# A decode kernel's query weight loaded in three pieces that split the 128 rows into 16 and 112, and a bias loaded in one transfer

## The chip, the cores and the metric

The kernel runs on one core of one Trainium2 chip. The metric is device time in microseconds of one execution, the median over several runs. A profile is taken of one execution; its "span" reaches from the first to the last instruction and is a little shorter than the time of the execution.

The core has five engines with queues of their own: PE (matrix multiply), DVE (vector), ACT (scalar functions), POOL and SP. SP and ACT also issue transfers (DMAs) between device memory and the on-chip memory, which has 128 rows (partitions). The transfers are carried out by 16 DMA engines.

## What is computed

One decode step of a block that adds attention over a sliding window of cached keys and values and a squared-ReLU MLP to its input. The batch is 2, one token each, the model width 576.

```python
xn = layernorm(x)                                   # 2 x 576
# attention: 32 query heads on 16 key/value heads of width 128
q = xn @ wq                                         # 576 x 4096
k, v = k_cache[:, :, Sk-W:], v_cache[:, :, Sk-W:]   # last W = 2048 of 8192 places
o = softmax(q k^T / sqrt(128)) v
att = o @ wo                                        # 4096 x 576
# MLP
h = relu(xn @ w1 + b1) ** 2                         # 576 x 4608
mlp = h @ w2 + b2                                   # 4608 x 576
out = x + att + mlp
```

All tensors are bf16. Each weight and each cached byte is used once, 53.6 MB in all.

## The kernel before

**The work.** The cache is cut into eight units: four groups of four key/value heads, for each of the two batch entries. A unit's keys are one load of 128 rows x 16,384 B (2 MB, `load_k`), its values another (`load_v`). `step(u)` transposes the unit's keys on PE (`transposes`), copies them out of PSUM on ACT and DVE (L273, L275), multiplies them with the queries (`scores`), and takes the softmax; the product with the values of unit `u - 2` (`pv`) is put between the transposes. The loop over `u` runs from 2 to 6, with `mlp_h` (the first half of the MLP) ahead of the last step.

**The weights.** `issue_flat` loads a weight as one flat run of bytes, cut into 128 equal rows: row p of the tile holds the p-th part. For wq a row is 18,432 elements, 36,864 B. `q_rows` multiplies in 36 matmuls, nine values of `t` times four of `g`; the matmul for `t` reads the columns from `2048 t` to `2048 t + 2047` of all 128 rows. wq, w1 and wo take turns in one buffer (`wbig`, one buffer).

**Order of the transfers.** All large loads go through SP's queue in this order: wq (two pieces, columns 0 to 4095 and 4096 to 18,431), k_0, k_1, v_0, k_2, v_1, k_3, then v_2 and k_4 and so on as buffers come free (six buffers for keys and values, so v_2 takes the place of k_0), w1 after v_5, wo after `mlp_h`, and at the end w2 in five pieces. ACT's queue has the small ones: x at the start, b1 (two transfers of four rows each, L420) and b2 (L421). b1 is wanted only in `mlp_h`, b2 in the first `out_acc`.

**What orders an issue.** The instruction stream of each engine is put in order by a scheduler: the b1 and b2 issues, which are written after the first softmax, stand in ACT's stream ahead of the `rstd` activation. Each transfer reports its end on one of eight counters, handed out in turn over all queues. A transfer's issue waits until the transfer that had the counter before it has landed, and, where it takes over a buffer, until the last reader of the old contents is done. In the kernel before, the counters 0 to 7 go to x, wq's first piece, wq's second piece, b1's first half, b1's second half, b2, k_0 and k_1; then v_0, k_2, v_1 and k_3 have counters 0 to 3. So k_2 is issued after the landing of wq's first piece, v_1 after that of the second, and k_3 after b1's first half.

Of the kernel before, what the change touches and what calls it, by code (L numbers as in the profile page):

```python
# [16 lines left out]
def kernel(  # L17
# [14 lines left out]
    nc = tc.nc  # L32
    P = 128
# [75 lines left out]
    def load_k(u):  # L109
        issue_kv(k_tiles, A_k_cache, u, "k")  # L110
# [1 line left out]
    def load_v(u):  # L112
        issue_kv(v_tiles, A_v_cache, u, "v")

    def issue_flat(w, name, cuts=()):
        n = w.shape[0] * w.shape[1] // P
        tl = wbig.tile([P, NH * L1], BF16, tag="wbig", name=name)
        w_p = w.rearrange("r n -> (r n)").rearrange("(p l) -> p l", p=P)
        for lo, hi in zip((0,) + cuts, cuts + (n,)):
            nc.sync.dma_start(out=tl[:, lo:hi], in_=w_p[:, lo:hi])  # L120
        return tl

    const.tile([P, 152], F32, name="pad_0")
# [4 lines left out]
    nc.vector.memset(eps_t[:], 1e-5)  # L128
    warm = const.tile([B, 2], F32, name="warm")
    nc.scalar.activation(out=warm[:, 0:1], in_=eps_t[:], func=ACT.Sqrt)  # L130
    wq_sb = issue_flat(A_wq, "wq", (4096,))
    load_k(0)
    load_k(1)
    load_v(0)
# [45 lines left out]
    for t0, half, k0, n, pc in ((0, 0, 0, NK, 0), (0, 1, 0, NK, 1), (1, 0, 1, NK - 1, 1), (1, 1, 0, NK - 1, 0)):  # L180
# [11 lines left out]
                          in_=own[:].unsqueeze(2).to_broadcast([P, NC, WC]))  # L192
# [11 lines left out]
                          in_=ident[0:2 * NG4, 0:2 * NG4].rearrange("p (x g) -> p x g", g=NG4).unsqueeze(3)  # L204
                          .to_broadcast([2 * NG4, 2, NG4, B]))

    b1_sb = const.tile([2 * NG4, HW], BF16, name="b1_sb")
# [208 lines left out]
    softmax(0)  # L416
    load_v(2)
    b1_rows = B_b1.rearrange("(x n) -> x n", n=HW)
    for i0, i1 in ((0, 4), (4, 8)):
        nc.scalar.dma_start(out=b1_sb[i0:i1, :], in_=b1_rows[i0:i1, :])  # L420
    nc.scalar.dma_start(out=xb_sb[B:B + 1, :], in_=B_b2.rearrange("(o n) -> o n", o=1))  # L421
    step(1)
    load_k(4)
# [1 line left out]
    for u in range(2, NU - 1):  # L425
        step(u)
        if u + 1 < NU - 2:
            load_v(u + 1)
        if u == 4:
            w1_sb = issue_flat(B_w1, "w1")  # L430
        if u + 3 < NU:
            load_k(u + 3)
        if u == 5:
            for v in (NU - 2, NU - 1):
                load_v(v)
    mlp_h(w1_sb)
    wo_sb = issue_flat(A_wo, "wo")
    w2a_sb = w2pool.tile([P, FR * D], BF16, name="w2a")
    w2b_sb = kvpool.tile([P, R9 * D], BF16, tag="kv", name="w2b")
# [28 lines left out]
    for r in range(FR):  # L468
        w, o = (w2b_sb, r) if r < R9 else (w2c_sb, r - R9)
# [41 lines left out]
```

## Time and profile before

| | us |
|---|---|
| median of 3 runs (133.61 to 133.85) | 133.74 |
| the profiled execution | 133.6 |
| its span | 131.7 |
| busy in the span: PE / DVE / ACT | 84.6 / 63.1 / 46.6 |
| wq's first piece: issue to landing | 4.8 |
| wq's second piece: issue to landing | 12.9 |
| a key load, median: issue to landing | 25.6 |
| mean granted TensorE clock (1 is full) | 0.883 |

The span holds 53.74 MB of DMA traffic, a mean of 408 GB/s. In the profile a line such as "L93 PE MATMUL q_ps<-wq,xnT 128*4 128x512 bf16 x28" names the line of the code (L93 and L96 are the helpers through which all matmuls and transposes go), the engine, the operation, the output and inputs, the shape and the number of instructions. "SPq" and "ACTq" are issues of transfers on those queues. The chain of waits is followed back from the last instruction to what released it. In the table of stretches, "1.50:2.00 0.50" is a stretch and its length; then come the busy time and count of each engine, the granted clock, the mean busy share of the 16 DMA engines and the GB/s. A packet is counted in one stretch, so shares over 1 occur in short ones.

### The profile page before, as it was taken

The numbers are of one execution on the slowest core, as the hardware profiler recorded it, in microseconds if no ns is written. First come the engines' busy times: TensorE is split into PE (matmuls) and PEld (weight loads), VectorE is DVE, ScalarE is ACT, GpSimd is POOL, SyncE is SP. The second block draws the span as 40 slices with busy tenths as digits, with TensorE's granted clock in tenths as the row PEclk, the third lists the DMA queues.
The fourth block names the chain that finished last, engine by engine and source line by source line (L and its number), as shares of the span: only waits on it lengthen the run. The fifth ranks groups of instructions, "written<-read, shape, count | busy, mean of one in ns | idle before, by whom it ended". The sixth has DMA issues, their size and how long they took to land.

```text
span 131.7 us, 2025 instructions
## 1 busy us (share of the span) xinstructions
PE 84.6 (64%) x818; PEld 46.3 (35%) x818; DVE 63.1 (48%) x176; ACT 46.6 (35%) x68; POOL 4.2 (3%) x14
## 2 busy tenths in 40 slices
PE   0040767985599687699687797003919974629782
PEld 0010236553346353345353353002507631205341
DVE  6760034555447677457677496400073487560000
ACT  6700019497255185265085283200015452000101
POOL 2000000010100100100100100100010001000000
PEclk9999999999779999859999999955586899655799
DMA  4999999999999999999999999999999989899970
GB/s 118 480 419 420 418 443 418 448 418 423 445 413 438 423 443 428 413 458 413 443 423 411 458 490 403 408 431 428 413 443 418 504 381 504 382 416 403 400 286 1
DMA packets 3643, 53.74 MB, mean 408 GB/s; under 512 B 418, under 2 KB 563, under 8 KB 819
## 3 DMA queue, kind: packets, MB, share of 16 engines
q1 hardware_dynamic: 3604, 53.61, 95.6%
q8 instruction: 6, 0.10, 0.3%
q10 hardware_dynamic: 30, 0.02, 0.0%
q14 instruction: 3, 0.02, 0.0%
HBM read 53.62 MB, written 0.00 MB: 407 GB/s over the span
## 4 chain that ended last, share of the span: by engine, by line
DMA 74%; PE 15%; ACT 5%; issue 1%; SPq 1%; DVE 1%; ACTq 0%; DVEq 0%
DMA w<-in_B_w_dram 24%; DMA w2c<-in_B_w_dram 23%; DMA k<-in_A_k_cache_dram 17%; DMA wq<-in_A_wq_dram 10%; PE kT_ps L96 5%; PE h_ps L93 3%; ACT kT L273 3%; PE q_ps L93 2%; PE sc_ps L93 2%; PE o_ps L93 1%; PE out_ps L93 1%; ACT L305 1%; SPq L120 1%; DVE qrow L241 1%; ACT qrow L241 0%
## 5 line engine op out<-in xcount | busy, mean ns | idle before, releaser
L96 PE MATMUL kT_ps<-ident_f,k 128*128 128x128 f32 x256 | 39.0, 295 | 6.7 <-DMA k<-in_A_k_cache_dram 4.2
L273 ACT COPY kT<-kT_ps 128x1024 bf16<-128x1024 bf16 x32 | 31.8, 1012 | 15.3 <-PE kT_ps L96 15.3
L96 PEld LDWEIGHTS kT_ps<-ident_f,k 128*128 128x128 f32 x256 | 29.3, 149 | 21.8 <-issue 7.4
L275 DVE COPY kT<-kT_ps 128x1024 bf16<-128x1024 bf16 x32 | 21.8, 682 | 6.4 <-PE kT_ps L96 5.9
L93 PE MATMUL sc_ps<-kT,qz 128*32 128x512 bf16 x128 | 9.8, 384 | 6.1 <-DVE kT L275 5.5
L305 ACT ACTIVATE p<-sc_ps,bias 128x512 bf16<-128x512 f32 x8 | 5.5, 687 | 21.5 <-DVE gown L301 21.4
L93 PE MATMUL o_ps<-v,pT 128*32 128x512 bf16 x128 | 12.2, 466 | 0.0
L93 PE MATMUL h_ps<-w,xnT 128*4 128x288 bf16 x72 | 4.5, 442 | 8.8 <-DMA w<-in_B_w_dram 8.8
L93 PEld LDWEIGHTS <-xnT 128*4 128x4 bf16 x108 | 3.5, 117 | 18.3 <-issue 15.3
L336 DVE SCALAR_TENSOR_TENSOR o<-o_ps,in_s,o 128x128 f32<-128x128 f32 x24 | 8.2, 344 | 0.4
L308 DVE STREAM_TRANSPOSE pT<-p 128x512 bf16<-128x512 bf16 x8 | 5.7, 709 | 5.6 <-ACT p L305 5.6
L376 DVE TENSOR_TENSOR hrow<-t 100x1152 bf16<-100x1152 f32 x2 | 2.6, 1354 | 10.5 <-ACT t L374 10.5
L93 PE MATMUL q_ps<-wq,xnT 128*4 128x512 bf16 x36 | 4.2, 622 | 5.4 <-DMA wq<-in_A_wq_dram 4.0
L294 DVE TENSOR_REDUCE m<-sc_ps 128x1 f32<-128x512 f32 x8 | 5.5, 691 | 3.4 <-PE sc_ps L93 3.4
L93 PE MATMUL op_ps<-o,of_h 128*32 128x129 f32 x16 | 3.4, 299 | 4.6 <-DVE o L336 4.6
L298 POOL PARTITION_ALL_REDUCE gmax<-m x8 | 2.9, 365 | 92.2 <-DVE m L296 92.2
L93 PEld LDWEIGHTS <-qz 128*32 128x32 bf16 x128 | 2.0, 94 | 9.9 <-DVE kT L275 7.6
L334 DVE TENSOR_SCALAR o<-o_ps,in_s 128x128 f32<-128x128 f32 x8 | 2.7, 343 | 5.3 <-PE o_ps L93 5.3
L96 PE MATMUL pro_ps<-ident,xn_sb 2*128 2x2 bf16 x5 | 0.9, 181 | 6.8 <-DVE xn_sb L171 6.5
L241 ACT CAST qrow<-q_ps 100x512 bf16<-100x512 f32 x1 | 0.6, 585 | 12.1 <-DVE qrow L241 12.1
L463 ACT COPY pre_sb<-pre_ps 34x288 f32<-34x288 f32 x1 | 0.4, 393 | 12.6 <-PE pre_ps L93 12.6
L93 PE MATMUL out_ps<-wo,ws 128*2 128x288 bf16 x32 | 4.0, 441 | 1.1 <-DVE ws L352 1.1
(76 smaller groups left out, 61.4 us busy)
## 6 DMA issues: line engine op xcount, KB each, us to landing
k<-in_A_k_cache_dram SPq DMA_DIRECT2D x8, 2048.0 KB, 25.6
v<-in_A_v_cache_dram SPq DMA_DIRECT2D x8, 2048.0 KB, 22.8
w<-in_B_w_dram SPq DMA_DIRECT2D x1, 5184.0 KB
wo<-in_A_wo_dram SPq DMA_DIRECT2D x1, 4608.0 KB
wq<-in_A_wq_dram SPq DMA_DIRECT2D x1, 3584.0 KB, 12.9
w2a<-in_B_w_dram SPq DMA_DIRECT2D x1, 2592.0 KB
w2b<-in_B_w_dram SPq DMA_DIRECT2D x1, 1296.0 KB, 29.2
wq<-in_A_wq_dram SPq DMA_DIRECT2D x1, 1024.0 KB, 4.8
```

The lines of the kernel that those rows point to most:

```text
L93: tc.keep_in_program_order(nc.tensor.matmul(*a, **k))
L96: tc.keep_in_program_order(nc.tensor.transpose(*a, **k))
L241: cp(out=qrow[:, k * QW:(k + 1) * QW].rearrange("p (i a d) -> p i a d", a=2, d=Dh), in_=q_ps[0:RB, k * QW // 2:(k + 1) * QW // 2].rearrang ...
L273: nc.scalar.copy(out=kT, in_=kT_ps[:])
L275: nc.vector.tensor_copy(out=kT, in_=kT_ps[:])
L294: nc.vector.tensor_reduce(out=m1[:], in_=sc_ps[:], axis=AX.X, op=ALU.max)
L298: nc.gpsimd.partition_all_reduce(gmax[:], m2[:], channels=P, reduce_op=ReduceOp.max)
L305: nc.scalar.activation(out=p_sb[:], in_=sc_ps[:], func=ACT.Exp, bias=bias[:, 0:1], scale=scale, accum_out=o1[:, Dh:Dh + 1])
L308: nc.vector.transpose(out=pT[:].rearrange("p j r -> p (j r)"), in_=p_sb[:])
L334: nc.vector.tensor_scalar(scalar1=in_s[:, 0:1], scalar2=None, op0=ALU.mult, **kw)
L336: nc.vector.scalar_tensor_tensor(scalar=in_s[:, k:k + 1], in1=o1[:, 0:Dh], op0=ALU.mult, op1=ALU.add, **kw)
L376: nc.vector.tensor_tensor(out=h4[:, :, k * HB:(k + 1) * HB], in0=t4, in1=t4, op=ALU.mult)
```

## The change

`issue_flat` takes a pair (rows, columns) in place of a list of cuts. With it, a weight is loaded in three transfers: the first columns of the first rows, then all columns of the other rows, then the rest of the first rows. wq uses (16, 8192), that is 16 rows x 16,384 B, 112 rows x 36,864 B, and 16 rows x 20,480 B. w1 and wo are loaded as before, in one transfer each. b1's eight rows come in one transfer in place of two.

```diff
-    def issue_flat(w, name, cuts=()):
+    def issue_flat(w, name, lead=None):
         n = w.shape[0] * w.shape[1] // P
         tl = wbig.tile([P, NH * L1], BF16, tag="wbig", name=name)
         w_p = w.rearrange("r n -> (r n)").rearrange("(p l) -> p l", p=P)
-        for lo, hi in zip((0,) + cuts, cuts + (n,)):
-            nc.sync.dma_start(out=tl[:, lo:hi], in_=w_p[:, lo:hi])
+        pieces = [(0, P, 0, n)]
+        if lead:
+            p1, c1 = lead
+            pieces = [(0, p1, 0, c1), (p1, P, 0, n), (0, p1, c1, n)]
+        for p0, p1, c0, c1 in pieces:
+            nc.sync.dma_start(out=tl[p0:p1, c0:c1], in_=w_p[p0:p1, c0:c1])
         return tl
...
-    wq_sb = issue_flat(A_wq, "wq", (4096,))
+    wq_sb = issue_flat(A_wq, "wq", (16, 8192))
...
-    for i0, i1 in ((0, 4), (4, 8)):
-        nc.scalar.dma_start(out=b1_sb[i0:i1, :], in_=b1_rows[i0:i1, :])
+    nc.scalar.dma_start(out=b1_sb[:], in_=b1_rows[:, :])
```

In the built program the counters 0 to 7 now go to x, wq's first piece, b1, b2, wq's second piece, wq's third piece, k_0 and k_1. v_0, k_2, v_1 and k_3 again have counters 0 to 3, so k_2 is issued after the landing of wq's first piece, v_1 after b1's and k_3 after b2's. The first matmul of `q_rows` waits for wq's first and second pieces, the seventeenth for the third. The order of the transfers on SP's queue, and all counters from v_2 on, are as before.

## The prediction

> **What bounds the kernel now.** I read the chain of waits first, then the DMA row of the slices, then the stretches of the start and the groups in order of time at both ends.
>
> ```profile
> DMA 74%; PE 15%; ACT 5%; issue 1%; SPq 1%; DVE 1%; ACTq 0%; DVEq 0%
> ...
> DMA  4999999999999999999999999999999989899970
> ```
> ```profile
> q1 hardware_dynamic: 3604, 53.61, 95.6%
> ...
> q10 hardware_dynamic: 30, 0.02, 0.0%
> ```
> Three quarters of the chain that ended last is transfers, and after the first 3.3 us slice the 16 DMA engines are busy in every slice until the work runs out. SP's queue (q1) alone fills 95.6% of them. So the kernel is one stream of 53.6 MB. Its two ends:
>
> ```profile
> 1.18 12.89 DMA wq<-in_A_wq_dram
> ...
> 14.12 3.18 PE q_ps L93 x28
> ...
> 96.95 30.81 DMA w2c<-in_B_w_dram
> ```
> The last weight piece lands at 127.75 us. After it come 1.36 us of matmuls (L470), a 0.39 us copy and the store. Whatever delays the stream delays the end by as much; whatever merely happens earlier on PE or ACT does not move it. The stretches (last two columns: DMA share, GB/s) give the stream's speed:
>
> ```profile
> 1.50:2.00 0.50, 0.00 (x0) 0.00 (x0) 0.44 (x3) 0.50 (x1) 0.00 (x0) 1.00 1.34 185
> 2.00:2.50 0.50, 0.00 (x0) 0.00 (x0) 0.43 (x4) 0.50 (x1) 0.00 (x0) 1.00 0.37 82
> 2.50:3.00 0.50, 0.00 (x0) 0.00 (x0) 0.47 (x3) 0.48 (x3) 0.00 (x0) 1.00 0.73 279
> ...
> 14.00:34.00 20.00, 15.66 (x132) 8.84 (x131) 8.95 (x19) 10.87 (x16) 0.36 (x1) 1.00 1.01 432
> ```
> Full speed is 432 GB/s. From 1.5 to 3.0 us it is 185, 82 and 279, in all 0.273 MB in 1.5 us.
>
> How rows go to engines follows from the packet counts. SP issues 25 transfers of 128 rows and one of 2 rows (the store): 25 x (128 + 16) + 2 + 2 = 3604, so a 128-row transfer is one packet a row and 16 completion writes, one an engine. ACT's queue (q10) moves 2 + 4 + 4 + 1 + 2 + 2 = 15 rows in 30 packets: each row has a completion of its own. A transfer of four rows therefore runs on four engines, one row each, and not on one engine that owns eight neighbouring rows.
>
> **The change, part by part.** Call the three wq pieces A (16 rows x 16,384 B = 262,144 B), B (112 rows x 36,864 B = 4,128,768 B) and C (16 rows x 20,480 B = 327,680 B). The bytes are those of before, 4.72 MB. By the counts above I take A and C as one row an engine and B as seven rows an engine (an estimate; 16 divides both). What is new is the pattern: sixteen engines writing sixteen neighbouring rows at once, and engines that each hold seven neighbouring rows, so that they no longer stand in eight fixed rows each. No row of the trace shows a large transfer that is narrower than 128 rows, so each cost is bounded from the stretches.
>
> A: in the trace the first 262,144 B take 1.5 us less the time of the last 11 KB of the 0.273 MB, about 1.45 us. Low end: one packet an engine in place of two, the whole ramp gone, 0.262 / 432 = 0.61 us, which is 0.84 less. High end: all of it at the slowest half microsecond, 82 GB/s, 3.20 us, which is 1.75 more. Taken: the mean of the first microsecond, (185 + 82) / 2 = 133 GB/s, since A is that stretch: 1.97 us, +0.5.
>
> C: low end 0.328 / 432 = 0.76 us, no loss. High end 82 GB/s, 4.0 us, +3.24. Taken: 133 GB/s, the stretch in which few bytes are under way on each engine, as in C: 2.46 us, +1.7.
>
> B: low end 4.129 / 432 = 9.56 us, as before. High end the half microsecond at 279 GB/s, the mildest of the three slow ones, since B is wide: 14.8 us, +5.2. No row is nearer to one end, so the middle: +2.6.
>
> Sum of the pieces: 0.5 + 1.7 + 2.6 = +4.8 us. There is nothing to absorb it, as the stream is full from 3.0 us to the last landing.
>
> The page "SBUF — State Buffer" of the Trainium skill, section "Door 1: The DMA port swizzle (why `[64,N]` ≈ `[32,N]`)", speaks against the change: how fast a transfer writes depends on how many of 16 ports its partitions reach, and partitions 0 to 15 reach four, for which it measured 104 GB/s. By it A and C, 589,824 B, would take 5.67 us where 432 GB/s gives 1.37, a loss of 4.3 us as an estimate from that page, and the sum with B unharmed would be 137.9. No run here shows it yet.
>
> Edits that cost nothing, each with its cover:
>
> ```profile
> 9.10 1.02 PE L93 MATMUL q_ps<-wq,xnT 128*4 128x512 bf16 x8 [1.37 <-DVE q_ps L225]
> ...
> 14.09 0.54 SPq L105 DMA_DIRECT2D v<-in_A_v_cache_dram  x1
> 14.67 0.60 SPq L105 DMA_DIRECT2D k<-in_A_k_cache_dram  x1
> ...
> 24.19 0.54 SPq L105 DMA_DIRECT2D v<-in_A_v_cache_dram  x1
> ```
> PE's early matmuls. Eight of 36 ran at 9.10 while the second piece was under way. Now the first sixteen wait for A and B, the last twenty for C. At 3.18 / 28 = 0.114 us each, 20 follow C's landing, 2.27 us in place of 3.18, and only if the sixteen (1.8 us) are done by then. That is 0.9 us to be won on PE, not on the stream: the first issue that needs it is v_2 at 24.19, which waits for PE to be done with k_0, and at that time the queue still holds 12.58 MB less (24.19 - 14.08) x 0.432 = 8.2 MB, 19 us of work.
>
> SP's third wq issue: about 0.40 us (two took 0.86), so k_0 is issued at some 2.05 in place of 1.64. wq's bytes cover it until 14.
>
> The completion counters. The program has eight, taken in turn, and a transfer's issue waits for the counter's last user. In the built program k_2 still waits for the first wq piece (A), but v_1 no longer waits for the second wq piece (the issue at 14.09): it waits for the b1 transfer, and k_3 for b2. The total is the same, so from v_2 on each waits as before. Behind those two issues on SP stand only further cache loads. At 14.09 the queue holds four loads, 8.39 MB or 19.4 us, so neither an earlier issue nor one late by up to 19 us moves the stream.
>
> The bias: one issue for two on ACT.
> ```profile
> 4.31 1.28 ACT L165 ACT_TABLE_LOAD   x1
> 4.58 0.61 ACTq L420 DMA_DIRECT2D b_sb<-in_B_b_dram  x2
> 5.22 0.27 ACTq L421 DMA_DIRECT2D xb_sb<-in_B_b_dram  x1
> 5.61 0.29 ACT L165 ACTIVATE rstd<-mv,eps_t 2x1 f32<-2x1 f32 x1
> ```
> The 0.3 us saved lies under the table load that ends at 5.59. Without that cover it would bring rstd 0.3 us earlier, and then the early q matmuls, which now wait for wq anyway. b1 is read at 81.8 us.
>
> Forecast: 133.6 (the profiled execution: span 131.7 and 1.9 around it) + 4.8 = 138.4. The median of the runs shown is 0.14 above that execution, so **138.5**.
>
> **The rivals.**
>
> Faster: the ramp. If narrow writes run at full speed, C and B cost nothing, and A alone decides. For it: the 82 GB/s at 2.0 to 2.5 us, with eight rows queued on each engine; a single packet an engine could come to speed sooner. Against it: the first packet's wait is there whatever its size. Half the ramp's 0.84 us: 133.6 - 0.4 + 0.14 = 133.3 (132.9 to 133.45). It decides as soon as C's 0.33 MB takes less than about 0.9 us.
>
> No change: the bytes, the engines and each engine's share (16,384 + 7 x 36,864 + 20,480 = 8 x 36,864 B) stay, the stream runs at 432 GB/s, and all else lies under it: 133.7. For it: every piece on SP's queue, from 0.15 MB (the last w2c) to 5.3 MB (w1), keeps the stream full. Against it: all those are 128 rows wide.
>
> Slower by more than I say: every doubtful term at its high end, 1.75 + 3.24 + 5.2 = 10.2, gives 143.8; it needs engines to collide through all of B.
>
> That the change does not do what it says is ruled out by the built program, which has the three pieces and the one bias transfer.
>
> **How the numbers follow.** A measurement here can tell 0.2%, 0.27 us, from no change. Forecast (slower) 0.62, its own range 135.0 to 142.0: the taken A and C with nothing for B give 133.74 + 2.2 = 135.9, of which I allow a mis-sizing of 0.9; the top is B at its high end with A and C as taken, 141.1, and as much again. The worst sum (slower too) 0.08, the ramp (faster) 0.20, no change 0.10. The predicted time is that of the likeliest. From 133.2 to 142.0 some 0.08 is left out above and some 0.10, half of the faster case, below.
>
> **What would show it.** Queue 1 with 3604 - 288 + (16 + 16) + (112 + 16) + (16 + 16) = 3508 packets if rows are dealt as I say; 3484 if A and C stay on four engines. Slow stretches of DMA, well under 432 GB/s, up to wq's last landing, which moves from 14.08 to about 18.9 and takes w2c's landing from 127.75 to about 132.5 with it. From then on 432 GB/s and the same distances between landings. If wq lands at 14 or sooner, the terms for B and C were wrong; if it lands late but w2c does not, the claim that the stream has no slack was.

## The result, and the profile after

The changed kernel took 143.93 us (median of 6 runs, 143.4 to 144.3) against 133.73 us before (6 runs, 133.53 to 133.85): the ratio is 1.0762, with a 95% interval of 1.0747 to 1.0777. It is slower by 10.2 us, and the prediction of 138.5 us with a range up to 142.0 missed it.

The rate by slices of the kernel before (3.29 us each), and of the kernel after (3.55 us each) the DMA row, the rate, the packets of SP's queue and the chain of waits:

```profile
GB/s 118 480 419 420 418 443 418 448 418 423 445 413 438 423 443 428 413 458 413 443 423 411 458 490 403 408 431 428 413 443 418 504 381 504 382 416 403 400 286 1
```
```profile
DMA  9969997999999999999999999999999999899970
GB/s 178 228 177 324 260 170 175 424 424 443 438 424 427 429 424 424 438 434 429 434 420 424 436 443 490 409 437 403 415 434 424 446 451 467 374 431 423 399 296 3
...
q1 hardware_dynamic: 3508, 53.61, 95.8%
...
DMA 79%; PE 11%; ACT 3%; issue 2%; SPq 2%
```

The DMA digits are nearly as high as before, yet for the first seven slices, some 25 us, the engines move 170 to 324 GB/s. Before, they moved 418 to 480 from the second slice on. The busy digit hardly shows this: a packet under way counts as busy however slowly it moves. Only the GB/s row does. The 3508 packets are the number worked out beforehand, so A, B and C are each spread over sixteen engines: one row an engine for A and C, seven for B. Which rows each engine got, the count does not say.

The stretches of the kernel after (busy time of PE, PEld, DVE, ACT and POOL, the clock, then the DMA share and GB/s):

```profile
5.00:8.00 3.00, 0.90 (x5) 0.49 (x5) 1.99 (x11) 0.91 (x2) 0.00 (x0) 1.00 0.84 197
8.00:11.00 3.00, 0.00 (x0) 0.00 (x0) 0.87 (x5) 0.00 (x0) 0.00 (x0) 1.00 1.21 347
11.00:14.00 3.00, 0.00 (x0) 0.00 (x0) 0.00 (x0) 0.00 (x0) 0.00 (x0) 1.00 0.93 246
14.00:17.00 3.00, 0.00 (x0) 0.00 (x0) 0.00 (x0) 0.00 (x0) 0.00 (x0) 1.00 0.90 209
17.00:20.00 3.00, 0.00 (x0) 0.00 (x0) 0.00 (x0) 0.00 (x0) 0.00 (x0) 1.00 0.94 218
20.00:24.00 4.00, 1.38 (x16) 0.54 (x17) 0.00 (x0) 0.00 (x0) 0.00 (x0) 1.00 0.96 151
...
34.00:80.00 46.00, 36.92 (x328) 21.04 (x327) 29.26 (x71) 25.05 (x32) 1.83 (x5) 0.96 1.01 429
```

From 5 to 20 us the stream is almost all B; these rows count a packet, bytes and busy time, in the stretch in which it starts, so single stretches swing. From 34 us on the speed is about that of before (429 GB/s; 439 in the same stretch before). The issues with their times to landing, and the two ends in the chain of waits:

```profile
wq<-in_A_wq_dram SPq DMA_DIRECT2D x1, 4032.0 KB, 21.3
...
wq<-in_A_wq_dram SPq DMA_DIRECT2D x1, 320.0 KB, 23.1
...
wq<-in_A_wq_dram SPq DMA_DIRECT2D x1, 256.0 KB, 4.6
```
```profile
1.64 0.43 SPq L124
...
106.92 31.18 DMA w2c<-in_B_w_dram
```

C, issued at 1.64, lands 23.1 us later, at 24.7; before, wq's last landing was at 14.08. That is 10.7 us. The w2c piece for which the last matmuls wait lands at 106.92 + 31.18 = 138.10 in place of 127.75, 10.35 us later. So the whole loss is there once wq has landed, and all but 0.3 us of it reaches the end.

The packets of the two traces give the size of each term. The table has the mean duration of a packet over the sixteen engines, one after the other as an engine carries them, and so the sum for one engine.

| per engine | before, us | after, us | difference |
|---|---|---|---|
| first 16,384 B | 0.83 + 0.35 (two packets) | 1.24 (A) | +0.06 |
| seven rows of 36,864 B | 7 x 1.364, the packet of wo, also 36,864 B | 3.05 + 2.52 + 2.09 + 2.00 + 2.30 + 2.53 + 2.42 = 16.91 (B) | +7.36 |
| 20,480 B | 0.76 (at 432 GB/s) | 2.13 (C) | +1.37 |
| the first two packets of k_0 | 2 x 0.611 | 1.82 + 0.80 | +1.40 |

The sum is 10.2 us, as measured. Each row holds what was under way at that time: what A costs the packets behind it stands in B's row, in the 3.05 us of B's first packets.

### The profile page after: what moved, and what is told of

The parts are those of the page before. It is cut to its first block, busy times and chain, and to the rows that moved or that the text cites. A ratio compares the mean times of both kernels' runs of the same rounds, so it can differ in the third digit from the quotient of the medians.

```text
span 142.1 us, 2025 instructions
## 1 busy us (share of the span) xinstructions
PE 84.8 (60%) x818; PEld 48.1 (34%) x818; DVE 63.2 (45%) x176; ACT 46.7 (33%) x68; POOL 4.2 (3%) x14
## 3 DMA queue, kind: packets, MB, share of 16 engines
q1 hardware_dynamic: 3508, 53.61, 95.8%
## 4 chain that ended last, share of the span: by engine, by line
DMA 79%; PE 11%; ACT 3%; issue 2%; SPq 2%
DMA k<-in_A_k_cache_dram 34%; DMA w<-in_B_w_dram 23%; DMA w2c<-in_B_w_dram 22%; PE kT_ps L96 6%; PE h_ps L93 3%; ACT kT L277 2%; SPq L124 1%; PE o_ps L93 1%; PE out_ps L93 1%; ACT L309 1%; PE sc_ps L93 1%; SPq L105 0%; SPq L443 0%; SPq L444 0%; ACT fin_sb L481 0%
## 5 line engine op out<-in xcount | busy, mean ns | idle before, releaser
L96 PE MATMUL kT_ps<-ident_f,k 128*128 128x128 f32 x256 | 40.1, 303 | 7.3 <-DMA k<-in_A_k_cache_dram 5.6
L96 PEld LDWEIGHTS kT_ps<-ident_f,k 128*128 128x128 f32 x256 | 30.9, 153 | 21.5 <-issue 11.5
L245 DVE CAST qrow<-q_ps 100x512 bf16<-100x512 f32 x1 | 0.7, 692 | 17.9 <-PE q_ps L93 17.9
```

The source lines that it names most:

```text
L96: tc.keep_in_program_order(nc.tensor.transpose(*a, **k))
```

## The experiments

Two theories were set against each other and against the counters. By the first, place: engines that write rows which share a write path slow each other, whatever the size of the transfer. The theory assumes that four neighbouring rows share one path, as rows 32 apart within the same half of 64 do, and that a path takes about one engine's full rate. By the second, the narrow or odd shape, or the addresses that the engines read, is what costs. `src_w1`, `one_narrow`, `halves` and `rows_32_96` were executed once each; the six executions of the changed kernel lie 0.9 us apart, so a difference below that says nothing there.

**The bias alone** (`bias_alone`): the kernel before with

```diff
-    for i0, i1 in ((0, 4), (4, 8)):
-        nc.scalar.dma_start(out=b1_sb[i0:i1, :], in_=b1_rows[i0:i1, :])
+    nc.scalar.dma_start(out=b1_sb[:], in_=b1_rows[:, :])
```

> The kernel before with b1 in one transfer, wq in its two wide pieces. My theory: the whole loss sits in the narrow pieces, so 133.7 +- 0.4. Rival (the counters): one transfer fewer shifts the counters, v_1 and k_3 wait for others; if that is what costs, 136 or more.

133.63 us against 133.57, ratio 1.0005 (0.9994 to 1.0017). The bias and the shift of the counters cost nothing. The loss is in the load of wq.

**Other addresses to read** (`src_w1`):

```diff
+        w1_p = B_w1.rearrange("r n -> (r n)").rearrange("(p l) -> p l", p=P)
...
-            nc.sync.dma_start(out=tl[p0:p1, c0:c1], in_=w_p[p0:p1, c0:c1])
+            src = w1_p if lead and p1 == P else w_p
+            nc.sync.dma_start(out=tl[p0:p1, c0:c1], in_=src[p0:p1, c0:c1])
```

> As the changed kernel, but the 112-row piece reads rows 16 to 127 of w1 (row pitch 41,472 B in place of 36,864 B, 36,864 B of each), so the query is made from other numbers; on-chip rows and bytes are the same. Theory on the write side (engines that write neighbouring rows slow each other): 143.9 +- 0.7, packets of 36,864 B still about 2.3 us. Theory on the read side (the engines' addresses in device memory, 7 x 36,864 B apart, collide): the distance is now 7 x 41,472 B, and the time moves by more than 2 us, toward 135 to 140 if the collision goes.

143.73 us. If each engine is dealt seven rows in a row, the engines' addresses in device memory are now 290,304 B apart in place of 258,048 B, and the time is the same within the spread of the changed kernel. The distance between the addresses read did not set the loss; a pair of runs below that reads the same addresses settles more.

**The 16 rows in one piece** (`one_narrow`):

```diff
-            pieces = [(0, p1, 0, c1), (p1, P, 0, n), (0, p1, c1, n)]
+            pieces = [(0, p1, 0, n), (p1, P, 0, n)]
```

> wq in two pieces: rows 0 to 15 whole, then rows 16 to 127 whole; the split of the 16 rows into A and C is taken back. If the 112-row piece carries most of the loss (its packets took 2.0 to 3.1 us where 1.36 is the full speed): 141 to 144. If the three-fold split or the last 16-row piece carries it: 135 to 138.

144.57 us, a little over the expected band. Splitting the 16 rows in two is not what costs; loading the rows as 16 and 112 is.

**Halves** (`halves`):

```diff
-            pieces = [(0, p1, 0, c1), (p1, P, 0, n), (0, p1, c1, n)]
+            pieces = [(0, 64, 0, n), (64, P, 0, n)]
```

> wq as rows 0 to 63, then rows 64 to 127, four rows an engine, both pieces whole rows. Write side, by place of the rows (64 neighbouring rows reach half of the write paths): half speed, 4.72 MB at 216 GB/s is 21.8 us in place of 10.9, about 144.5. Read side: the engines' addresses are four rows apart as in a 128-row load, so about 133.7. If only a row count an engine that is not a multiple of four hurts: 133.7 too.

145.45 us, 1 us above the expected 144.5: two pieces of half the rows each, four rows an engine, and it is the slowest of all. In its stretches, the rate while wq is under way:

```profile
11.00:17.00 6.00, 0.00 (x0) 0.00 (x0) 0.00 (x0) 0.00 (x0) 0.00 (x0) 1.00 0.95 198
17.00:23.00 6.00, 0.00 (x0) 0.00 (x0) 0.00 (x0) 0.00 (x0) 0.00 (x0) 1.00 0.99 203
```

Of its 128 packets 96 took about 2.89 us, 12.8 GB/s an engine, a little under half of the 27 GB/s of a 128-row load (36,864 B in 1.364 us); the sixteen at the start of each half took 2.57 and 2.73. This is the cleanest case, and what the first theory expects: two engines on each write path, each at half speed. That the engines stood so is its assumption; the trace names no engine's rows.

**32 and 96 rows** (`rows_32_96`):

```diff
-            pieces = [(0, p1, 0, c1), (p1, P, 0, n), (0, p1, c1, n)]
+            pieces = [(0, 32, 0, n), (32, P, 0, n)]
```

> wq as rows 0 to 31 (two an engine), then rows 32 to 127 (six an engine). By place: the first piece on eight paths, 1.18 MB at 205 GB/s, 5.8 us in place of 2.7, +3.0; the second reaches all paths but not one engine to each; if it is slowed as the 112 rows were (2.4 in place of 1.36 us a packet), 6 x 1.0 = +6.2, in all 143. If only seven rows an engine (an odd share) were slow: 136.8.

144.18 us, 1.2 above what place gave. Two or six rows an engine are no better than seven; an odd share is not the cause. Nearly all packets took 2.4 to 2.9 us (119 of 128).

**The same bytes in other places.** These runs have wq wide and the bias in one transfer; in the middle of the stream, behind k_3, two additional loads go to w2a's tile, which is overwritten later. Only the rows they are written to differ; the loads of eight rows also have half the bytes, on half the engines (the comments name the run):

```diff
+    nc.sync.dma_start(out=w2a_sb[:, 0:1296], in_=w2_p[:, 0:1296])            # ex_wide
+    nc.sync.dma_start(out=w2a_sb[:, 1296:2592], in_=w2_p[:, 1296:2592])
...
+    nc.sync.dma_start(out=w2a_sb[0:16, :], in_=w2_p[0:16, :])                # ex_near16
+    nc.sync.dma_start(out=w2a_sb[16:32, :], in_=w2_p[16:32, :])
...
+    nc.sync.dma_start(out=w2a_sb[0:128:8, :], in_=w2_p[0:16, :])             # ex_far16
+    nc.sync.dma_start(out=w2a_sb[1:128:8, :], in_=w2_p[16:32, :])
...
+    nc.sync.dma_start(out=w2a_sb[0:8, :], in_=w2_p[0:8, :])                  # ex_near8
+    nc.sync.dma_start(out=w2a_sb[8:16, :], in_=w2_p[8:16, :])
...
+    nc.sync.dma_start(out=w2a_sb[0:32:4, :], in_=w2_p[0:8, :])               # ex_far8
+    nc.sync.dma_start(out=w2a_sb[32:64:4, :], in_=w2_p[8:16, :])
```

> Control for the next two: wq and all else as in the kernel before with b1 in one transfer, and two additional loads of 128 rows x 2,592 B (663,552 B in all, never read) in the middle of the stream, behind k_3. At 432 GB/s they take 1.5 us: 135.2 +- 0.5 by every theory.

> The same number of bytes as the control, as two loads of 16 neighbouring rows x 20,736 B (rows 0 to 15, then 16 to 31). The two halves of the run with rows 0 to 63 gave 12.8 GB/s an engine, two engines on one write path of 25.6. By place of the rows, 16 neighbouring rows are four paths, 102 GB/s: 6.5 us in place of 1.5, so 140.2 +- 0.7. If being narrow costs only at the start, where nothing else is under way: 135.2.

> As the previous run, but the 16 rows of a load lie eight apart (0, 8, ..., 120, then 1, 9, ..., 121): as many rows, engines, packets and bytes, other places. By place: eight paths with two engines each, 205 GB/s, 3.2 us in place of 1.5, so 136.9 +- 0.5. If one row an engine, or 16 rows as such, is what costs: the same time as with neighbouring rows.

> Wide wq, b1 in one transfer, and in the middle of the stream two additional loads of 8 rows x 20,736 B whose rows lie four apart (0, 4, ..., 28, then 32, 36, ..., 60). Eight engines carry them, 41,472 B each, as much for each of these engines as in the wide control. By place: no two of the eight engines write rows of one path, packets of 20,736 B at the full 0.77 us, 135.4 +- 0.6 as the control. If narrow loads are slow in themselves: 138 or more.

> As the previous run with neighbouring rows (0 to 7, then 8 to 15). By place: four engines on each of two paths, 6.4 GB/s an engine, 6.5 us in place of 1.5: 140 +- 0.8. If only the number of rows counts: the same time as with rows four apart.

| | rows | bytes an engine that takes part | median, us | ratio to before (95%) |
|---|---|---|---|---|
| ex_wide | 128 | 41,472 | 135.48 | 1.0129 (1.0099 to 1.0158) |
| ex_far8 | 8, four apart | 41,472 | 135.07 | 1.0116 (1.0096 to 1.0137) |
| ex_near8 | 8, neighbours | 41,472 | 138.22 | 1.0352 (1.0326 to 1.0379) |
| ex_far16 | 16, eight apart | 41,472 | 138.10 | 1.0325 (1.0292 to 1.0358) |
| ex_near16 | 16, neighbours | 41,472 | 140.07 | 1.0472 (1.0417 to 1.0528) |

Each has two executions; those with 128 or 16 rows load 663,552 B in all and stand against 133.77, `ex_far8` and `ex_near8` half of that, on eight engines, against 133.47.

The same eight rows of w2, read from the same addresses, cost 3.2 us more when they are written side by side than four rows apart. That pair leaves the read side out: only the rows written differ. Written four apart, they cost what an engine's share of 41,472 B takes in the wide control, 1.6 against 1.7 us. Neither being narrow nor one row an engine slows a packet in itself; that only eight engines work does mean 1.6 us for half of the control's bytes. The stretches of `ex_near16`, of `ex_far8` and of `ex_near8` over the same time:

```profile
42.00:44.00 2.00, 1.22 (x14) 0.66 (x14) 1.48 (x4) 1.01 (x1) 0.00 (x0) 1.00 1.43 291
44.00:46.00 2.00, 0.38 (x8) 0.00 (x0) 0.96 (x3) 0.00 (x0) 0.37 (x1) 0.96 1.10 133
46.00:48.00 2.00, 0.00 (x0) 0.00 (x0) 0.85 (x3) 0.78 (x2) 0.00 (x0) 0.50 0.70 101
```
```profile
42.00:44.00 2.00, 1.22 (x14) 0.61 (x14) 1.46 (x4) 1.01 (x1) 0.00 (x0) 1.00 1.10 471
44.00:46.00 2.00, 1.75 (x24) 0.98 (x16) 1.01 (x3) 0.00 (x0) 0.36 (x1) 1.00 0.99 424
```
```profile
42.00:44.00 2.00, 1.22 (x11) 0.68 (x14) 1.42 (x4) 1.01 (x1) 0.00 (x0) 1.00 1.46 333
44.00:46.00 2.00, 0.43 (x8) 0.00 (x0) 0.98 (x3) 0.00 (x0) 0.37 (x1) 0.82 0.85 129
```

With neighbouring rows the whole stream falls to 101 to 133 GB/s, and PE (the first busy time in the line) runs dry beside it; with rows four apart the rate stays at full speed. In `ex_far8` all packets under way at that time took 0.771 us (20,736 B) or 0.611 us (16,384 B), full speed.

In `ex_near8` only eight engines carry the 16 narrow packets (3636 packets on SP's queue in place of 3604: eight rows and eight completions for each of the two loads). The other eight go on to v_2, and still their 16,384 B packets took up to 1.8 us. Which rows of v_2 they wrote is not in the trace. But eight neighbouring rows in one load and eight in the next are four paths by the theory's assumption, and by it each engine of a 128-row load at full speed must stand on a path of its own; so at most four engines can have met the crowded rows directly, and all were slowed. That the crowding spreads to engines that write elsewhere is argued from this count. Two misses have to do with this. `ex_far16` cost 1.2 us more than expected: most of the narrow packets of its second load took 1.53 to 1.59 us, as the 1.6 worked out, but the 16,384 B packets beside them took 1.02 us on average in place of 0.611, and what all of these lost comes to 1.4 us an engine. `ex_near8` cost 1.8 us less than expected: its narrow packets took 1.67 us on average where place gave 3.2. They lost 0.9 us an engine, and the 16,384 B packets 2.5. Why is left open.

**The first piece alone** (`front16`), wide wq behind it:

```diff
+    nc.sync.dma_start(out=w2a_sb[0:16, 0:8192], in_=w2_p[0:16, 0:8192])
     wq_sb = issue_flat(A_wq, "wq", (4096,))
```

> The first narrow piece alone: an additional load of 16 rows x 16,384 B ahead of a wide wq (b1 in one transfer, the data never read). At full speed 0.6 us more than the kernel with the bias change alone (133.6): 134.2, and my prediction's price of A, +0.5, gives 134.7. By place, 102 GB/s: 2.6 us more, 136.2, less what lies under the ramp of the start (0.8 at most): 135.4 to 136.2.

135.01 us against 133.47, ratio 1.0114 (1.0097 to 1.0131): 1.54 us for 262,144 B that take 0.61 at full speed, so 0.93 us is A's price. That is a miss for both values worked out, 134.7 and 135.4 to 136.2; it lies between them.

**The first columns wide** (`wide_then_narrow`):

```diff
+            pieces = [(0, P, 0, c1), (p1, P, c1, n), (0, p1, c1, n)]
```

> wq's first 16,384 B of all 128 rows, then the other 20,480 B of rows 16 to 127, then those of rows 0 to 15. The first narrow piece is gone and the 112-row piece is 0.56 of its size. In the changed kernel a packet of the 112 rows took 2.42 us in place of 1.36, one of the last 16 rows 2.13 in place of 0.76, and the first packet of k_0 1.82 in place of 0.61. If these prices go with bytes: 0.56 x 7.4 = 4.1, 1.4 and 1.2 more: 133.7 + 6.7 = 140.4 +- 0.7. If the first narrow piece set the engines against each other and the rest follows from it: 136 or less.

139.31 us, ratio 1.0434 (1.0413 to 1.0454): 5.8 us of loss where 6.7 was expected, 0.4 below the band. A is gone and B is 0.56 of its size. B's packets of 20,480 B took 1.21 us in place of 0.76, 3.2 us an engine; C lost 1.35 and the first packets of k_0 1.31. These sum to 5.9, so the same account holds here; the first piece did not set off the rest.

No run points to a version faster than the kernel before: every cut of wq by rows lost time.

## Why the prediction was wrong

What bounds the kernel: right. The stream has no slack, and a delay of 10.7 us at wq's landing arrives as 10.35 us at w2c's. One reading was off without harm: the landing at 127.75 is that of w2c's first piece (864 KB), not of the last weight piece. The packets of the two small pieces behind it end at 128.48, under the last matmuls, and after the change at 138.84, 10.36 later too.

How many engines a load uses: right, by the packet count of 3508. Which rows each gets stayed an assumption.

The edits priced at nothing: right. The bias alone made no difference, and PE in the changed kernel ran sixteen q matmuls at 22.62 and twenty at 24.82, the latter 2.05 us long, behind the landings and under the stream.

A, "+0.5": 0.93 measured alone.

C, "+1.7": its packets lost 1.37, and the first packets of k_0 behind it another 1.40. The prediction had no term for what comes behind a narrow piece. Together 2.77, within the ends it gave for C (0 to 3.24).

B, "+2.6", the middle between nothing and 5.2: this is the step that failed. It lost 7.36 us an engine. A's share in that, since the first B packets wait behind A's writes, is about the 0.93 above at most; what is left, 6.4, still lies beyond the high end. In `wide_then_narrow`, without A ahead of it, 0.56 of B lost 3.2; by bytes that is 5.7 for all of B, an estimate, and still above 5.2. The bound was "the half microsecond at 279 GB/s, the mildest of the three slow ones, since B is wide". B ran at 4.13 MB / 16.9 us = 244 GB/s, through all of its 16.9 us and not for a stretch. I took a piece of 112 rows for almost harmless because it is wide. What counts, by the runs with eight and sixteen rows, is where the rows lie that are written at the same moment. That this is also what slows 112, 96, 64 and 32 rows is the reading that fits all of these runs: `src_w1` and `rows_32_96` speak against the rivals tried, the distance read and the odd share. It also fits the trace of the changed kernel, in which the packets of all sixteen engines are slow in each of the seven rounds (none under 1.83 us, 1.364 at full speed). Which rows of the 112 each engine was dealt, no run shows, and so the size of 7.4 us is measured, not derived.

The source of all three prices was wrong as well. They came from the stretches between 1.5 and 3.0 us, and those count a packet's bytes where it starts. In the changed kernel the first of them reads

```profile
1.50:2.00 0.50, 0.00 (x0) 0.00 (x0) 0.44 (x3) 0.50 (x1) 0.00 (x0) 1.00 1.59 332
```

though its first wq packet ends at 2.49. Spread over the packets' durations, the kernel before moved 32, 126 and 253 GB/s in the three stretches that read 185, 82 and 279. So these are figures of the start of a 128-row load; that A and C came out near their prices is luck.

The rival "slower by more" gave 143.8, but by a wrong sum, so the hit is luck: its high ends for A (1.75) and C (3.24) were too high, and that for B (5.2) too low. Its condition, engines colliding through all of B, fits the slow packets in all seven rounds.

The page "SBUF — State Buffer" of the Trainium skill, section "Door 1: The DMA port swizzle (why `[64,N]` ≈ `[32,N]`)", gave 104 GB/s for partitions 0 to 15. The nearest run is `one_narrow`: its 589,824 B for rows 0 to 15 were under way from 1.75 to 7.29 us, 106 GB/s, though B's first packets ran beside the end of it. The 262,144 B of `front16` took 1.75 to 3.38 us, 161 GB/s, so a short load does not show that limit. For partitions 0 to 63, eight ports, the page measured 196; `halves` shows 198 to 203. So its table agrees with the two longer loads; read as "how many ports are reached" it says nothing against 112 rows, and there the measurement decides. The page "DMA: Bandwidth & Descriptors", section "Back-pressure in remote DMA", says of transfers between cores that a saturated port on the receiving side clogs the way back to the engines that write to it and to any that share this way; the slowed v_2 packets of `ex_near8` look like that for a load from device memory, though no run shows which way is shared.

## What to carry to other kernels

A load that is cut by rows is not the same bytes in another order: it changes which rows are written at the same moment, and with it the speed: here by a factor of about two for half of the rows (packets of 2.89 us in place of 1.364) and three and a half for sixteen neighbours (2.7 in place of 0.77). Cut by columns and keep all 128 rows. In a profile, look for it in the GB/s row beside the DMA digits: the engines stay "busy", 0.94 at 218 GB/s. And a row of a short stretch is no speed where packets last longer than it.

## What the runs showed of the hardware that was not expected

- The slowing reaches other packets. While eight neighbouring rows were written, the eight engines that carried none of them needed up to 1.8 us for packets that take 0.611.
- It reaches the next load. The first sixteen packets of k_0, itself a 128-row load, ran beside C's last and took 1.82 us; the next sixteen, started from 23.67 on, when C's last packet was through, took 0.80.
- Eight rows four apart, on eight engines, ran at full speed (0.771 us for 20,736 B) beside a full stream.
